# One weight piece per attention iteration, and one listed tail with filler products, in a kernel of attention, soft mixture of experts and a cosine MLP

## The chip, the cores and the metric

The kernel runs on one core of a Trainium2 chip. The metric is device time in microseconds (us) of one execution, as the median of three runs. The engines are named as in the profile: PE is TensorE's matrix products, PEld its weight loads, DVE is VectorE, ACT ScalarE, POOL GpSimd, and SP is SyncE, whose instruction queue issues all the transfers of this kernel.

## The reference

Three stages follow each other; cut to what matters:

```python
scores = q @ k.T / 8, causal mask;  attn = softmax(scores);  x = attn @ v      # 4 x 12 heads, 448 x 64
x = x as (1792 tokens, 768)
logits = x @ phi                              # 1792 x 32, 8 experts of 4 slots
d = softmax(logits, over tokens);  slot_in = d.T @ x
slot_out[e] = relu(slot_in[e] @ w1[e]) @ w2[e]   # 8 experts, 768 -> 1024 -> 768
x = softmax(logits, over slots) @ slot_out
h = x @ w_in;  out = (h * cos(h)) @ w_out        # 768 -> 2048 -> 768
```

All inputs and the output are float32. The expert weights are 50 MB, and each is read once.

## The kernel before

**Attention.** The 48 heads are worked off as 24 pairs. The tuple ORDER names the steps of one iteration, each with a lag: at iteration t, step (op, lag) works on pair t - lag, so that four pairs are in flight. S0, S1, S2 and Q3 are the score products (lines 300 and 306), sc and e the masking and the exponential (322 and 324), n the division on POOL (343), T0 and T1 the transposes of the probabilities (346), PV the product with v (390), evo the copy of its result (190), X the transposes to token rows (402). At the end of each batch of six pairs come phiA and phiB (411, 417), the logits `lg`, their replication `rep` (426), the softmax over tokens with a running maximum (dmax, dexp, dlgD, dsum), its transposition `dk` (346, on tile dT), and u0, u1 (480), which add the batch to the experts' slot inputs in `uacc` (489).

**The tail** is what the steps yield from iteration 23 on, when no pair is left to start, followed by bs0 and bs1 (the slot inputs, divided and transposed, line 502), their copy `bsc` (505) and the zeroing of two PSUM banks, mz1 and mz2 (542). The step `slots` (515 to 517) makes the divisor that bs0 reads. Before the change all of it is generated from ORDER with its lags.

**Transfers.** `run_ops` issues them from SP as soon as a step has freed their place: q and k of pair p + 2 into a buffer of two (`load_raw`, line 250) after pair p's score products, v (`load_v`, 256) after its PV. The expert weights come in 48 pieces of 1 MB (`load_piece`, 265 and 268) through a ring of 26 slots; 19 of the slots are free during attention, the other seven when the last pair's buffers are done with (the table FREE). A piece is issued with each evo, and two with those of pairs 1 and 3, until 19 are under way:

```python
            if op == "evo" and len(pieces) < NPRE:
                load_piece()
                if i in (1, 3):
                    load_piece()
```

**Experts.** A second block with a manual schedule runs the eight experts in two groups: w1 (line 761) in two halves of six pieces, w2 (776) in three of four. Each piece that PE has used frees a slot for another. The softmax of the tokens over slots (`tok_softmax`, 465 to 471) and `build_ct`, which makes the MLP's operand CT from it, are called inside this block. Two bank memsets (608) stand between the blocks. `keep_warm` (493) is a product that nobody reads; it writes bank 3 from the constants `cs`. Some stand in the last w2 products.

**MLP.** The last pieces are followed on SP by the first raw chunks of w_in and w_out (`ld`, 682), which are unpacked by ACT and DVE (689 to 700; the second chunk by `decode(1)` ahead of the last copy on ACT, 782). A planner with listed costs then sets the order of the MLP (836 to 864), where PE is busy without a break.

Of the kernel before, what the change touches and what calls it, by code (L numbers as in the profile page):

```python
# [35 lines left out]
KW = 4  # L36
HEAD = None
TH = 2
TT = 23
TAIL = None  # L40
ORDER = (
# [126 lines left out]
def moe_stack_kernel(ctx: ExitStack, tc: tile.TileContext, qk, v, cst, phi, w1, w2, w_in, w_out, out):  # L168
# [16 lines left out]
    PE, ACT, DVE, POOL, SP = nc.tensor, nc.scalar, nc.vector, nc.gpsimd, nc.sync  # L185
# [12 lines left out]
    bank = [psum.tile([128, 512], F32, name=f"bank{i}") for i in range(8)]  # L198
    TA, TB, OB, MB = bank[4:8]
# [6 lines left out]
    pslot = [slot(f"p{i}") for i in range(2)]  # L206
# [4 lines left out]
    cs = fixed.tile([128, 832], F32, name="cs")  # L211
# [4 lines left out]
    mask0 = qks[:, 1920:1984]  # L216
    rep = cs[:, 640:768]
    phs = fixed.tile([128, NPB, NS], F32, name="phs")
    ctoks = fixed.tile([128, NB * 4, NS], F32, name="ctok")
    ctok = ctoks[0:112]  # L220
    uacc = fixed.tile([128, DM], F32, name="uacc")
# [3 lines left out]
    dk = fixed.tile([128, 4, NS], F32, name="dk")  # L225
# [4 lines left out]
    b_q = fixed.tile([128, 1], F32, name="b_q")  # L230
    b_h = fixed.tile([128, 1], F32, name="b_h")
# [15 lines left out]
    @pr("load_raw")  # L247
    def load_raw(p):
        b, hp = divmod(p, NPB)
        SP.dma_start(QK(p), qk[b, hp])  # L250

    @pr("load_v")
    def load_v(p):
        b, hp = divmod(p, NPB)
        for c, n, t in VB[p % 2]:
            SP.dma_start(t, v[b, hp][:, 128 * c:128 * (c + n)])
# [3 lines left out]
    def load_piece():  # L260
        i = len(pieces)
        g, r = divmod(i, 24)
        t = slot(f"w{i}")
        if r < 12:
            SP.dma_start(t, w1[g, r // 6, r % 6])
        else:
            r -= 12
            SP.dma_start(t, w2[g, r // 4, r % 4])
        pieces.append(t)
# [221 lines left out]
    def keep_warm(n, t=cs):  # L491
        for _ in range(n):
            PE.matmul(bank[3 if t is cs else 7][:, 0:128], lhsT=t[:, 0:128], rhs=t[:, 0:128], start=True, stop=True)
# [18 lines left out]
    def slots(b):  # L512
        if b < NB - 1:
# [6 lines left out]
                T0=lambda p: t_pair(p, 0), T1=lambda p: t_pair(p, 1), PV=pv, X=x_t, evo=ev_o)  # L520
# [9 lines left out]
    for e in "AD":  # L530
        for i in range(4):
            PAIR[f"ev{i}{e}"] = lambda p, i=i, e=e: ev_t(i, e)
        for j in range(2):
            PAIR[f"evx{j}{e}"] = lambda p, j=j, e=e: ev_x(p, j, e)
    BATCH = dict(phiA=phi_a, phiB=phi_b, lg=be_logits, rep=be_rep, dmax=d_max, dexp=d_exp, dlg=lambda b: d_lg(b, "A"),
                 dlgD=lambda b: d_lg(b, "D"), dsum=d_sum, dk=be_dk, dkc=dk_c, tokc=tok_c, slots=slots)
    for h in range(2):
# [4 lines left out]
                 mz1=lambda b: DVE.memset(bank[1], 0.0), mz2=lambda b: DVE.memset(bank[2], 0.0),  # L542
# [11 lines left out]
    def all_ops():  # L554
        yield from HEAD or steps(0, TH)
        yield from steps(TH, TT)
        yield from TAIL or (*steps(TT, NPAIR + 6), ("bs0", 3), ("bs1", 3), ("bsc", 3), ("mz1", 3), ("mz2", 3))

# [5 lines left out]
    def run_ops():  # L564
        done = set()
        raws, vs = [2], [2]
        ok = lambda p, xs: all((x, p) in done for x in xs)
        for op, i in all_ops():
            (PAIR if op in PAIR else BATCH)[op](i)
            done.add((op, i))  # L570
            while raws[0] < NPAIR and ok(raws[0] - 2, ("S0", "S1", "S2", "Q3")):
                load_raw(raws[0])
                raws[0] += 1
            while vs[0] < NPAIR and ok(vs[0] - 2, ("PV",)):
                load_v(vs[0])
                vs[0] += 1
            if op == "evo" and len(pieces) < NPRE:
                load_piece()
                if i in (1, 3):
                    load_piece()  # L580
            while NPRE <= len(pieces) < NSLOT and raws[0] == vs[0] == NPAIR and done.issuperset(FREE[len(pieces) - NPRE]):
                load_piece()

    with tc.manual_schedule():
        load_raw(0)
        SP.dma_start(cs[:, 128:832], cst[:, 128:832])
        SP.dma_start(mask0, cst[:, 832:896])
        SP.dma_start(cs[:, 0:128], cst[:, 0:128])
        load_raw(1)
        load_v(0)  # L590
        load_v(1)
        SP.dma_start(phs, phi)
        DVE.memset(TA, 0.0)
        DVE.memset(TB, 0.0)
        for i in range(2):
            DVE.memset(pslot[i][:, 1984:2048], 0.0)
        DVE.memset(b_q, 0.25)
        DVE.memset(b_h, 0.5 * math.pi)
        DVE.memset(uacc[:, 0:128], 0.0)
        keep_warm(KW, uacc)  # L600
        run_ops()


    hT = dk.rearrange("p c m -> p (c m)").rearrange("p (c m) -> p c m", c=8)
    h1 = cs[:, 128:640]
    so = cs[:, 384:640]
    for i in (4, 5):
        DVE.memset(bank[i][:, 0:256], 0.0)

    def build_ct():  # L610
        ct = ex["CT"]
        ACT.activation(st[0:112, 42:43], tst[:, 16:17], AF.Sin)
# [135 lines left out]
        return t  # L748

    with tc.manual_schedule():  # L750
        for g in range(2):
            for hf in range(2):
                hb = bank[1 + hf]
                for i in range(6):
                    if (g, hf, i) == (0, 0, 2):
                        tok_softmax()
                    if (g, hf, i) == (0, 1, 3):
                        build_ct()
                    w = next_piece().rearrange("p (j f) -> p j f", j=4)
                    for j in range(4):  # L760
                        PE.matmul(hb[32 * j:32 * j + 4, :], lhsT=slotT[:, i, 16 * g + 4 * j:16 * g + 4 * j + 4],  # L761
                                  rhs=w[:, j, :], start=(i == 0), stop=(i == 5))
                ACT.activation(h1, hb, AF.Relu)
                tb = bank[3 * hf]
                for c in range(4):
                    PE.transpose(tb[:, 128 * c:128 * c + 128], h1[:, 128 * c:128 * c + 128], ident)
                DVE.tensor_copy(hT[:, 4 * hf:4 * hf + 4, :].rearrange("p c (j t) -> p c j t", j=4),
                                tb.rearrange("p (c j t) -> p c j t", c=4, j=4)[:, :, :, 0:SPE])
            for n in range(3):
                sb = bank[4 + n % 2]  # L770
                for qd in range(4):
                    w = next_piece().rearrange("p (c j f) -> p c j f", c=2, j=4)
                    for c in range(2):
                        kc = 2 * qd + c
                        for j in range(4):
                            PE.matmul(sb[32 * j:32 * j + 4, 0:256], lhsT=hT[:, kc, 4 * j:4 * j + 4], rhs=w[:, c, j, :],  # L776
                                      start=(kc == 0), stop=(kc == 7))
                    if 42 <= npc[0] < 48:
                        keep_warm(3)
                if npc[0] == 48:  # L780
                    decode(1)
                ACT.activation(so, sb[:, 0:256], AF.Copy)
                tb = bank[6]
                if npc[0] == 48:
                    keep_warm(1)
                for c in range(2):
                    PE.transpose(tb[:, 128 * c:128 * c + 128], so[:, 128 * c:128 * c + 128], ident)
                DVE.tensor_copy(soT[:, 2 * n:2 * n + 2, 16 * g:16 * g + 16].rearrange("p c (j t) -> p c j t", j=4),
                                tb[:, 0:256].rearrange("p (c j t) -> p c j t", c=2, j=4)[:, :, :, 0:SPE])
# [339 lines left out]
```

## Time and profile before

| | before |
|---|---|
| runs, us | 527.07, 527.98, 528.55 (median 527.98) |
| profiled execution, us | 527.23, span 525.4 |
| mean granted TensorE clock | 0.972 |
| busy: PE, PEld, DVE, ACT, POOL | 93%, 68%, 66%, 60%, 37% |
| chain that ended last | PE 75%, DMA 8%, DVE 8%, ACT 5% |
| transfers | 100.35 MB, 191 GB/s over the span |
| expert pieces (48 x 1024 KB) | 7.3 us from issue to landing, median |
| q and k of a pair (24 x 480 KB) | 5.5 us from issue to landing, median |

The busy share is an average over stages with different limits: attention up to about 160 us, its tail to 183, the experts to 247, the MLP to the end. The chain gives for each stretch the instruction or transfer that was waited for. [...] A row of a timeline shows the start, the length of the group, engine, line, operation and tiles, the count, and in brackets the idle time of the engine just before with what ended it.

### The profile page before, as it was taken

What the parts mean: (1) busy time and instruction counts of PE and PEld (TensorE: products, weight loads), DVE (VectorE), ACT (ScalarE), POOL (GpSimd) and SP (SyncE); (2) the same over time, 40 slices, a digit from 0 to 9 for tenths busy, and PEclk for the clock granted to TensorE, in tenths of its full rate; (3) what the DMA queues carried; (4) which work ended last, traced back from release to release, by engine and by line L of the source; (5) the groups of instructions that cost most, each with busy time, mean ns of one, the idle gap of its engine ahead of it and who ended that gap; (6) DMA issues with size and microseconds to landing.
All of it is one profiled execution on the core that took longest, in us unless ns stands there. A gap on an engine that the chain in (4) does not pass through costs nothing.

```text
span 525.4 us, 11211 instructions
## 1 busy us (share of the span) xinstructions
PE 490.2 (93%) x4234; PEld 358.5 (68%) x4234; DVE 344.3 (66%) x877; ACT 314.0 (60%) x735; POOL 196.4 (37%) x299
## 2 busy tenths in 40 slices
PE   6988999999998598888888999999999999999996
PEld 4755677677675423334766878887877787888996
DVE  4766887887884613003888899897998886445431
ACT  5878989989985111001769665747566546543552
POOL 2654556566563000000236334243433456222331
PEclk9989999999999579999899999999999999999999
DMA  5688878877328789999443434333263011213101
GB/s 195 200 334 329 302 263 278 290 278 286 111 79 304 273 324 422 418 422 415 185 181 120 131 111 129 114 120 121 81 220 120 1 61 39 82 59 129 54 1 60
DMA packets 24244, 100.35 MB, mean 191 GB/s; under 512 B 2816, under 2 KB 6912, under 8 KB 18048
## 3 DMA queue, kind: packets, MB, share of 16 engines
q1 hardware_dynamic: 24192, 99.66, 51.7%
q8 instruction: 33, 0.54, 0.4%
q14 instruction: 19, 0.16, 0.1%
HBM read 94.14 MB, written 5.51 MB: 190 GB/s over the span
## 4 chain that ended last, share of the span: by engine, by line
PE 75%; DMA 8%; DVE 8%; ACT 5%; issue 2%; POOL 0%; SPq 0%; ACTq 0%; DVEq 0%
PE bank L862 12%; PE bank L864 12%; PE bank L863 12%; PE bank L390 9%; PE bank L306 7%; PE bank L346 5%; DMA zraw<-in_w_out_dram 5%; PE bank L761 4%; DMA qk<-in_qk_dram 3%; PE bank L836 3%; PE bank L776 2%; PE bank L480 1%; PE bank L803 1%; PE bank L300 1%; DVE zscr L843 1%
## 5 line engine op out<-in xcount | busy, mean ns | idle before, releaser
L862 PE MATMUL bank<-zg,zhl 128*128 128x512 f32 (+1 forms) x378 | 139.8, 370 | 0.4 <-ACT zhl L711 0.4
L863 PE MATMUL bank<-zg,zhl 128*128 128x512 f32 (+1 forms) x378 | 137.5, 364 | 0.9 <-DVE zhl L724 0.9
L864 PE MATMUL bank<-zg,zhl 128*128 128x512 f32 (+1 forms) x378 | 137.3, 363 | 0.9 <-POOL zg L855 0.9
L855 POOL TENSOR_TENSOR zg<-zscr,zg 128x512 fp32r<-128x512 f32 (+1 forms) x64 | 82.6, 1295 | 135.9 <-ACT zg L852 121.4
L343 POOL TENSOR_SCALAR p<-p,pst 128x448 f32<-128x448 f32 (+3 forms) x168 | 82.6, 502 | 48.8 <-DVE pst L335 28.2
L324 ACT ACTIVATE p<-p,pst 128x448 f32<-128x448 f32 (+3 forms) x168 | 87.8, 524 | 13.3 <-DVE pst L322 10.9
L862 PEld LDWEIGHTS bank<-zg,zhl 128*128 128x128 f32 x378 | 71.4, 189 | 13.7 <-issue 1.2
L864 PEld LDWEIGHTS bank<-zg,zhl 128*128 128x128 f32 x378 | 71.4, 189 | 12.6 <-POOL zg L855 1.3
L863 PEld LDWEIGHTS bank<-zg,zhl 128*128 128x128 f32 x378 | 71.5, 189 | 12.4 <-DVE zhl L724 1.6
L322 DVE CUSTOM_DVE_ANT_0 p<-bank,cs 128x448 f32<-128x448 f32 (+1 forms) x96 | 52.6, 548 | 14.9 <-PE bank L300 8.5
L843 DVE SCALAR_TENSOR_TENSOR zscr<-zscr,bank 128x512 f32<-128x512 int32 (+1 forms) x64 | 38.7, 617 | 32.4 <-ACT zscr L840 32.0
L846 ACT ACTIVATE zscr<-zscr,b_h 128x512 f32<-128x512 f32 (+1 forms) x64 | 42.0, 669 | 28.8 <-DVE zscr L843 28.5
L306 PE MATMUL bank<-qk 64*128 64x192 f32 (+2 forms) x288 | 54.2, 474 | 4.3 <-DMA qk<-in_qk_dram 4.3
L852 ACT ACTIVATE zg<-zscr 128x512 fp32r<-128x512 f32 (+1 forms) x64 | 36.3, 576 | 26.0 <-DVE zscr L849 25.9
L849 DVE TENSOR_TENSOR zscr<-bank,zscr 128x512 f32<-128x512 f32 (+1 forms) x64 | 39.1, 620 | 18.3 <-ACT zscr L846 18.3
L840 ACT ACTIVATE zscr<-bank,b_q 128x512 int32<-128x512 f32 (+1 forms) x64 | 39.4, 629 | 19.6 <-PE bank L836 19.5
L724 POOL TENSOR_TENSOR zhl<-uacc,zhl 128x768 fp32r<-128x768 f32 (+1 forms) x7 | 10.8, 1548 | 105.7 <-DMA zraw<-in_w_out_dram 90.5
L689 ACT ACTIVATE zraw<-zraw 128x768 f32<-128x768 f32 x32 | 29.2, 913 | 22.6 <-DMA zraw<-in_w_in_dram 11.2
L192 DVE COPY pts<-bank 128x512 f32<-128x512 f32 x48 | 32.9, 686 | 14.3 <-PE bank L346 14.2
L346 PE MATMUL bank<-cs,p 64*128 64x64 f32 (+1 forms) x768 | 36.6, 230 | 3.8 <-POOL p L343 2.0
L346 PEld LDWEIGHTS bank<-cs,p 64*128 64x128 f32 (+1 forms) x768 | 29.4, 136 | 12.9 <-issue 4.6
L306 PEld LDWEIGHTS bank<-qk 64*128 64x128 f32 x288 | 26.7, 198 | 9.2 <-DMA qk<-in_qk_dram 4.6
(145 smaller groups left out, 699.7 us busy)
## 6 DMA issues: line engine op xcount, KB each, us to landing
w<-in_w_dram SPq DMA_DIRECT2D x48, 1024.0 KB, 7.3
zraw<-in_w_in_dram SPq DMA_DIRECT2D x16, 768.0 KB, 4.4
zraw<-in_w_out_dram SPq DMA_DIRECT2D x16, 768.0 KB, 4.3
qk<-in_qk_dram SPq DMA_DIRECT2D x24, 480.0 KB, 5.5
xk<-in_v_dram SPq DMA_DIRECT2D x12, 256.0 KB, 2.9
out_dram<-zps SPq DMA_DIRECT2D x8, 256.0 KB, 3.7
xts<-in_v_dram SPq DMA_DIRECT2D x12, 128.0 KB, 2.5
lt<-in_v_dram SPq DMA_DIRECT2D x12, 128.0 KB, 2.8
```

What stands on the lines that cost most here:

```text
L306: PE.matmul(sreg(j, c), lhsT=Q(p)[h, q0:q0 + 128], rhs=K(p)[h, 0:ln], start=True, stop=True)
L322: DVE.tensor_tensor_reduce(out=dst, in0=sb, in1=m, scale=-0.125, scalar=3.0e38, op0=ALU.add, op1=ALU.min, accum_out=st_[:, col:col + 1])
L324: return pr(f"exp{j}{c}")(lambda: ACT.activation(dst, dst, AF.Exp, bias=st_[:, col:col + 1], scale=-1.0, accum_out=st_[:, 8 + col:9 + col]))
L343: POOL.tensor_scalar(dst, dst, st_[:, 24 + col:25 + col], 0.0, op0=ALU.mult, op1=ALU.add)
L346: PE.transpose(out, src, by)
L390: PE.matmul(OB[64 * j:64 * j + 64, a:b], lhsT=V(p, c, j), rhs=r[j], start=first, stop=last)
L843: DVE.scalar_tensor_tensor(y_(s), y_(s).bitcast(I32), -2.0 * math.pi, hb[:, 0:n_(s)], op0=ALU.mult, op1=ALU.add)
L846: ACT.activation(y_(s), y_(s), AF.Sin, bias=b_h, scale=1.0)
L855: eng.tensor_tensor(g_(s)[1], y_(s), g_(s)[0].bitcast(F32), ALU.subtract)
L862: PE.matmul(o, lhsT=wh, rhs=gh, start=first, stop=False)
L863: PE.matmul(o, lhsT=wl, rhs=gh, start=False, stop=False)
L864: PE.matmul(o, lhsT=wh, rhs=gl, start=False, stop=last)
```

## The change

Three edits. The extra pieces with pairs 1 and 3 go, so that each of the first 19 evo steps issues one piece, the last with pair 18 instead of 16. TAIL, which was None, now lists all steps from iteration 23 to the start of the experts by hand. In it `slots` of the last batch stands right behind `dsum`, and three groups of fillers are added: `kwc` 8 behind `rep`, `kwc` 3 behind `dk` and `kwc` 5 behind `u1`, 16 calls of keep_warm(1) in all. The helpers of the experts move up unchanged, and the memsets of banks 4 and 5 and the experts' loop now stand inside the first manual block, so that the two are one.

```diff
-TAIL = None
+TAIL = (
...
+    ("phiB", 3), ("evx0D", 23), ("lg", 3), ("rep", 3), ("kwc", 8), ("dmax", 3), ("dexp", 3), ("dlgD", 3), ("dsum", 3),
+    ("slots", 3), ("dk", 3), ("kwc", 3), ("dkc", 3), ("tokc", 3), ("u0", 3), ("ua0", 3), ("u1", 3), ("kwc", 5),
+    ("ua1", 3), ("bs0", 3), ("bs1", 3), ("bsc", 3), ("mz1", 3), ("mz2", 3))
...
             if op == "evo" and len(pieces) < NPRE:
                 load_piece()
-                if i in (1, 3):
-                    load_piece()
...
     with tc.manual_schedule():
...
         keep_warm(KW, uacc)
         run_ops()
-
-    for i in (4, 5):
-        DVE.memset(bank[i][:, 0:256], 0.0)
...
-    with tc.manual_schedule():
+        for i in (4, 5):
+            DVE.memset(bank[i][:, 0:256], 0.0)
         for g in range(2):
             for hf in range(2):
                 hb = bank[1 + hf]
```

The order of ACT and of POOL is the same as before. Three engines' orders move. (Line numbers of the changed kernel are its own: 262 is load_raw, 268 load_v, 277 load_piece.)

SP in the first iterations: qk is q and k of a pair, xk, xts and lt receive v, w_N is a weight piece. Before:

```order
L250 DMA qk<-in_qk_dram 128x960
L256 DMA xts<-in_v_dram 128x256
L256 DMA lt<-in_v_dram 128x256
L265 DMA w_337<-in_w_dram 128x2048
L265 DMA w_339<-in_w_dram 128x2048
L250 DMA qk<-in_qk_dram 128x960
L256 DMA xk_77<-in_v_dram 128x512
L265 DMA w_435<-in_w_dram 128x2048
```

and with the change:

```order
L262 DMA qk<-in_qk_dram 128x960
L268 DMA xts<-in_v_dram 128x256
L268 DMA lt<-in_v_dram 128x256
L277 DMA w_337<-in_w_dram 128x2048
L262 DMA qk<-in_qk_dram 128x960
L268 DMA xk_77<-in_v_dram 128x512
L277 DMA w_433<-in_w_dram 128x2048
```

One piece instead of two stands ahead of this load of q and k, and the same happens once more four rows on; two pieces stand two iterations later at the end of the row of 19.

PE from `rep` to the first expert product (bank_67 is bank 3, written by the fillers). Before:

```order
L426 MATMUL bank_71<-lt,cs 128x448
L346 MATMUL bank_71<-cs,dT 112x128 x4
L480 MATMUL bank_71<-xk_77,dk 32x128 x12
L480 MATMUL bank_69<-xk_78,dk 32x128 x12
L502 MATMUL bank_64<-pst_87,uacc 128x32 x6
L761 MATMUL bank_65<-w_240,phs 4x512 x4
```

and with the change (505 is keep_warm, each of these rows counts two passes on the engine):

```order
L438 MATMUL bank_71<-lt,cs 128x448
L505 MATMUL bank_67<-cs 128x128 x8
L358 MATMUL bank_71<-cs,dT 112x128 x4
L505 MATMUL bank_67<-cs 128x128 x3
L492 MATMUL bank_71<-xk_77,dk 32x128 x12
L492 MATMUL bank_69<-xk_78,dk 32x128 x12
L505 MATMUL bank_67<-cs 128x128 x5
L514 MATMUL bank_64<-pst_87,uacc 128x32 x6
L767 MATMUL bank_65<-w_240,phs 4x512 x4
```

Only the three groups of fillers are new; the order of the rest stands.

DVE from `dsum` on, where 515 to 517 are `slots`, 465 to 471 the softmax of the tokens over slots, 489 the additions to uacc, 505 the copy of the slot inputs. Before:

```order
L450 SCALAR_TENSOR_TENSOR st<-st 128x1
L457 COPY dk<-bank_71 112x128
L460 COPY ctok<-bank_71 112x128
L465 TENSOR_REDUCE pst_88<-ctok 112x16
L466 TENSOR_TENSOR ctok<-ctok,pst_88 112x512
L489 SCALAR_TENSOR_TENSOR uacc<-uacc,st,bank_71 128x384
L489 SCALAR_TENSOR_TENSOR uacc<-uacc,st,bank_69 128x384
L515 TENSOR_SCALAR st<-st 128x1
L468 TENSOR_REDUCE pst_88<-ctok 112x16
L516 RECIPROCAL st<-st 128x1
L608 MEMSET bank_69 128x256
L517 TENSOR_SCALAR pst_87<-cs,st 128x32
```

and with the change:

```order
L462 SCALAR_TENSOR_TENSOR st<-st 128x1
L527 TENSOR_SCALAR st<-st 128x1
L528 RECIPROCAL st<-st 128x1
L529 TENSOR_SCALAR pst_87<-cs,st 128x32
L469 COPY dk<-bank_71 112x128
L472 COPY ctok<-bank_71 112x128
L501 SCALAR_TENSOR_TENSOR uacc<-uacc,st,bank_71 128x384
L501 SCALAR_TENSOR_TENSOR uacc<-uacc,st,bank_69 128x384
L517 COPY phs<-bank_64 128x192
L554 MEMSET bank_65 128x512
L554 MEMSET bank_66 128x512
```

The divisor is made before the transposes are copied, and the tokens' softmax with its six instructions now comes behind the copy of the slot inputs and four memsets.

## Rows read from the trace of the kernel before

**Rows 1.** PE's waits from 12 to 60 us: in total, times, longest (us).

```profile
PE bank L306 <- DMA qk<-in_qk_dram: 4.3, 2, 2.3
```

**Rows 2.** Timeline of SP, its issues around 25 us (start, length).

```profile
24.89 0.99 SPq L265 DMA_DIRECT2D w<-in_w_dram  x2
26.07 0.33 SPq L250 DMA_DIRECT2D qk<-in_qk_dram  x1
```

**Rows 3.** The loads of q and k (line 250), whole span.

```profile
DMA to landing us min/median/max: 3.3/5.5/8.8
```

**Rows 4.** Timeline of PE: the first score product of pairs 5 and 7.

```profile
34.91 1.25 PE L306 MATMUL bank<-qk 64*128 64x448 f32 x4 [2.27 <-DMA qk<-in_qk_dram]
...
50.25 1.02 PE L306 MATMUL bank<-qk 64*128 64x448 f32 x4 [2.03 <-DMA qk<-in_qk_dram]
```

**Rows 5.** Busy time by stretch: length; PE to POOL; granted clock, DMA share, GB/s.

```profile
26.72:55.99 29.27, 24.97 (x327) 16.36 (x322) 19.25 (x87) 23.23 (x74) 15.92 (x37) 0.94 0.85 321
69.67:94.37 24.70, 24.70 (x347) 17.61 (x344) 19.91 (x89) 23.31 (x75) 15.94 (x37) 1.00 0.81 286
34.91:42.65 7.74, 7.74 (x83) 4.36 (x83) 3.63 (x17) 4.01 (x13) 2.59 (x6) 0.78 0.60 197
76.19:82.84 6.65, 6.65 (x87) 4.48 (x85) 5.58 (x27) 6.52 (x22) 4.53 (x10) 1.00 0.73 243
```

**Rows 6.** Timeline of PE, the tail from rep to the first expert product.

```profile
169.88 1.02 PE L426 MATMUL bank<-lt,cs 128*128 128x448 f32 x2 [0.66 <-ACT lt L422]
173.22 1.10 PE L346 MATMUL bank<-cs,dT 128*112 128x128 f32 x4 [2.32 <-DVE dT L192]
174.89 2.79 PE L480 MATMUL bank<-xk,dk 112*32 112x128 f32 x48 [0.58 <-DVE ctok L460]
179.55 2.77 PE L502 MATMUL bank<-pst,uacc 128*128 128x32 f32 x12 [1.87 <-DVE pst L469]
183.36 1.03 PE L761 MATMUL bank<-w,phs 128*4 128x512 f32 x4 [1.04 <-DVE bank L542]
```

**Rows 7.** Busy time by stretch in tail and experts, columns as in rows 5.

```profile
169.00:172.50 3.50, 1.23 (x10) 0.30 (x2) 1.00 (x3) 1.40 (x5) 0.00 (x0) 0.95 1.04 370
172.50:183.40 10.90, 6.70 (x68) 5.54 (x72) 6.86 (x19) 0.82 (x3) 0.00 (x0) 0.50 0.71 261
...
184.00:187.00 3.00, 3.00 (x20) 0.59 (x16) 0.00 (x0) 0.00 (x0) 0.00 (x0) 0.50 0.30 52
187.00:247.50 60.50, 54.37 (x640) 22.17 (x632) 10.50 (x26) 6.59 (x12) 0.00 (x0) 0.98 1.01 418
```

**Rows 8.** Timeline of SP: the pieces issued in the tail and at the experts' start.

```profile
176.46 1.64 SPq L265 DMA_DIRECT2D w<-in_w_dram  x2
...
185.30 2.04 SPq L265 DMA_DIRECT2D w<-in_w_dram  x2
```

**Rows 9.** The chain that ended last, and ACT's timeline, at the MLP's start.

```profile
228.19 19.34 DMA zraw<-in_w_out_dram
...
247.55 0.92 ACT L689 ACTIVATE zraw<-zraw 128x768 f32<-128x768 f32 x1 [7.63 <-DMA zraw<-in_w_out_dram]
```

**Rows 10.** Timeline of PE at the higher clock: dk, half of u, w1 pieces, fillers.

```profile
63.61 0.65 PE L346 MATMUL bank<-cs,dT 128*112 128x128 f32 x4
...
66.64 0.86 PE L480 MATMUL bank<-xk,dk 112*32 112x128 f32 x24
...
192.87 2.76 PE L761 MATMUL bank<-w,phs 128*4 128x512 f32 x24
...
255.88 1.39 PE L493 MATMUL bank<-cs 128*128 128x128 f32 x11
```

**Rows 11.** Timeline of DVE in the tail.

```profile
177.75 0.62 DVE L489 SCALAR_TENSOR_TENSOR uacc<-uacc,st,bank 128x384 f32<-128x384 f32 x1 [0.66 <-PE bank L480]
...
179.32 0.17 DVE L517 TENSOR_SCALAR pst<-cs,st 128x32 f32<-128x32 f32 x1
...
179.84 0.69 DVE L471 TENSOR_TENSOR ctok<-ctok,pst 112x512 f32<-112x512 f32 x1
```

More of the change, by code (lines that the diff above doesn't have):

```diff
@@ L578, in run_ops @@
                 load_piece()
-                if i in (1, 3):
-                    load_piece()
             while NPRE <= len(pieces) < NSLOT and raws[0] == vs[0] == NPAIR and done.issuperset(FREE[len(pieces) - NPRE]):
                 load_piece()
-    with tc.manual_schedule():
[L585 to L601, printed above, removed]
     hT = dk.rearrange("p c m -> p (c m)").rearrange("p (c m) -> p c m", c=8)
@@ L750, in moe_stack_kernel @@
     with tc.manual_schedule():
+        load_raw(0)
+        SP.dma_start(cs[:, 128:832], cst[:, 128:832])
+        SP.dma_start(mask0, cst[:, 832:896])
+        SP.dma_start(cs[:, 0:128], cst[:, 0:128])
+        load_raw(1)
+        load_v(0)
+        load_v(1)
+        SP.dma_start(phs, phi)
+        DVE.memset(TA, 0.0)
+        DVE.memset(TB, 0.0)
+        for i in range(2):
+            DVE.memset(pslot[i][:, 1984:2048], 0.0)
+        DVE.memset(b_q, 0.25)
+        DVE.memset(b_h, 0.5 * math.pi)
+        DVE.memset(uacc[:, 0:128], 0.0)
+        keep_warm(KW, uacc)
+        run_ops()
+        for i in (4, 5):
+            DVE.memset(bank[i][:, 0:256], 0.0)
         for g in range(2):
```

9 rows, old and new, of the table TAIL are left out of this document.

## The prediction, made before the changed kernel was run

> **What bounds the kernel now.** PE is busy 93% of the span, so I looked first for the stretches where it is not, or where its clock is down. There are two. The list of PE's waits shows, in the first 60 us, one releaser that isn't an engine: the score products waited twice for a load of q and k, 4.3 us in all [rows 1]. SP's timeline says why: two weight pieces of 1 MB were issued 1.2 us ahead of that load [rows 2], which then took 8.8 us to land, the longest of the 24, against a median of 5.5 [rows 3]. PE's timeline puts the waits ahead of pairs 5 and 7 [rows 4], the first pairs loaded after the two double issues (pairs 1 and 3).
>
> The second stretch is the tail. [...] PE's timeline shows a chain of small steps, each waiting for DVE: dk 2.32 us, u 0.58, the slot products 1.87, the experts 1.04 [rows 6].
>
> What makes these waits count is the stage behind them. From 187 to 247.5 us the DMA engines are full at 418 GB/s [rows 7], and the MLP starts when the second raw chunk lands: it was issued at 228.19, landed 19.34 us later behind pieces still under way, and ACT had waited 7.63 us for it [rows 9]. So between tail and MLP the kernel is bound by transfers, and a faster tail helps by as much as it starts that stream earlier. The stream starts when PE has used its first piece: the issue at 185.30 [rows 8], 1.94 us after the first expert product at 183.36 [rows 6]. Just before, from 184 to 187, the DMA share was 0.30 [rows 7]: there the queue was short of work, so an earlier issue is not wasted. From the MLP on nothing is edited, and I let it move as a block.
>
> **The front: one piece instead of two.** From the first score product of pair 4 to that of pair 8 took 29.27 us, at a clock of 0.94. The same places in the next batch, pairs 10 to 14, took 24.70 at clock 1.00 [rows 5], and they hold 0.86 us of u1 products [rows 10] that the first batch doesn't have: 23.84 us. The difference is **5.4 us**. It can be worked out the other way: the two waits, 2.27 + 2.03 [rows 4], and the lower clock behind the first, 7.74 us from pair 5 to 6 against 6.65 one batch later [rows 5], 1.1: again 5.4. The batches behind already issue one piece per iteration and show no such wait, which is why I take all of it. The check on pair 5: PE was ready for it at 34.91 - 2.27 = 32.64, which is 6.6 us after the issue at 26.07; with one piece ahead the median landing is 5.5 [rows 2, 3], so 1.1 us are spare. Bounds: 4.3 if the clock's share isn't saved, 5.4 at most. SP also issues one transfer less ahead of those loads; that is inside the 5.4. The two pieces put off go out with pairs 17 and 18, in iterations that had none, where they meet what other iterations carry without waiting (DMA share 0.81, clock 1.00 [rows 5]); they are used some 40 us later. I cost them at nothing; if they made one qk late, it would cost about 2 us once.
>
> **The tail.** All times are those of the trace before, without the front's shift. `rep` ends at 170.90 [rows 6]. A filler is two passes of 1.39 / 11 = 0.126 us at the higher clock [rows 10].
> - Eight fillers take 2.0 us and end at 172.9, inside the 2.32 us that PE waited for DVE: dk still starts at 173.22. They cost nothing and keep PE at work. At the higher clock dk takes 0.65 instead of 1.10 [rows 6, 10] and ends at 173.9.
> - Three fillers, 0.8 us, end at 174.6. Meanwhile DVE copies dk and ctok, 0.6 us. So u starts at 174.6, 0.2 later than it could, and still 0.3 earlier than before.
> - u0 and u1 take 2 x 0.86 = 1.7 instead of 2.79 [rows 6, 10]: done at 176.35. The two pieces that wait for their buffers move from 176.46 [rows 8] to about 175.6.
> - Five fillers, 1.3 us, end at 177.6, while DVE adds, 0.62 each, until about 177.0 [rows 11]. They hold the slot products up by 0.6.
> - Before, those waited till 179.5 for the divisor (L517 at 179.32), which stood behind instructions of the tokens' softmax although uacc was ready at 178.37 [rows 11]. Now the divisor is made right behind `dsum`, in time in which DVE waits for dk. So they start at 177.65. Twelve passes at 0.126 are 1.5 us instead of 2.77 [rows 6]: done at 179.15 instead of 182.32.
> - The copy and the first memset stay, 1.04 us [rows 6]: the experts start at 180.2, 3.2 earlier. A first piece of eight passes takes 8 x 2.76 / 24 = 0.9 us [rows 10], and the next issue comes about 1.1 us after the start instead of 1.94: at 181.3, **4.0 us** earlier.
>
> From this I take off 0.3 us, because the two pieces of 176.46 move only 0.9 and now run into the new ones: **3.7 us**. Bounds: 3.2, what the experts' start alone gives, and 4.4, if the fillers between cost nothing. The tokens' softmax, now behind the memsets, has four DVE instructions about as long as L471's 0.69 us [rows 11], two small ones and one on ACT: some 4 us under the first six pieces, which take PE 48 x 2.76 / 24 = 5.5 us [rows 10]; nothing waits for it before build_ct's transposes, three pieces later. The memsets of banks 4 and 5 lie there too, long before w2 uses them. If that cover failed, the first copy behind it on DVE would come late by the overhang, and PE, which runs ahead of the transfers here, could lose that.
>
> PE itself must follow. Its experts started 3.2 earlier and the first half gains the lower clock's share on top, so it is ahead of the transfers by more than before, and they stay the bound. What is late next is the second raw chunk, as now [rows 9].
>
> **Sum.** 5.4 + 3.7 = 9.1 us off. The profiled execution took 527.23, 0.75 under the median of the runs; against it the sum is 518.1. The four executions shown have a mean of 527.7, and I take that as the base of a median: **518.6 us**. The forecast's own range goes from 516.6 (5.4 and 4.4, and 1 us for the spread of executions) to 520.6 (4.3 and 3.2, with the same).
>
> **Rivals.**
> - *The clock falls before the first filler.* Between 168 and 170.9 PE has gaps of its own, 0.66 us among them [rows 6]. If the clock is down when the fillers start, they take double, 4 us, and push dk to 174.9; with the durations of rows 6 the slot products end at 185.6, and the stream starts 3.2 us later than before: 525.5 if it stays down throughout. But PE now works without a break, and after the fall behind pair 5 the clock was back within the iteration (0.78 over it [rows 5]); if it returns halfway, the tail comes out about even: 522. Against it speaks that the clock fell only after 1.7 us of idleness behind `rep` had joined the earlier gaps [rows 6, 7]. [...] Chance 0.12.
> - *One wait in front stays.* The spare 1.1 us are less than the landing times scatter [rows 3]. One wait with its clock is 2.3 + 1.1: 522.0. Chance 0.08.
> - *The tail's gain ends at another wait*, because the stream is not what the MLP waits for once it comes earlier, or PE takes its place: 527.7 - 5.4 = 522.3. Against it: 7.63 us of ACT's waiting [rows 9]. Chance 0.05.
> - *Slower: one piece per iteration is already too much.* Without the waits the pairs follow faster, and if every load of q and k then lands later than the 6.6 us that are there, PE waits in each of some 17 iterations, the front gains nothing, and each microsecond over costs 17. It breaks even with the tail's 3.7 at a landing of 6.8 us; at 7.5 us it is 527.7 - 3.7 + 15.3 = 539. Against it: iterations from 56 us on do carry a piece each, at full clock and without a gap [rows 5], with a median landing of 5.5 [rows 3]. Chance 0.02.
>
> **How the numbers follow.** The forecast has 0.73. The range of 8 in 10 reaches from its lower end over most of the cases that give 522: 516.6 to 522.0. Outside lie the clock that stays down, the slower rival, and some scatter. A measurement of this kernel can tell about 0.3%, 1.6 us, from no change; all cases but the last give more than that unless two come together: faster 0.95, same 0.03, slower 0.02.
>
> **What would show it.** Right: no wait of PE for q and k in the first 60 us, and 23.5 to 24.5 us from pair 4 to pair 8 at clock 1.00; granted clock 1.00 from rep to the experts, dk at 0.65 and the u products at 1.7 us; the slot products starting at uacc and not at the divisor; from the end of rep to the first expert product 9.3 us instead of 12.5; the DMA engines full from about 1 us after that; the second raw chunk landing about 9 us earlier, and the MLP as long as before. Wrong: a clock of 0.50 anywhere between rep and the first half of w1, fillers of 0.5 us, qk landings over 6.6 us with a wait behind, or a raw chunk that lands earlier while ACT or DVE start on it no sooner.

## The result, and the profile after

The changed kernel takes **521.6 us** (median of four runs, 521.30 to 521.62), beside 528.3 for the kernel before, measured with it: a ratio of 0.9875, 95% interval 0.9857 to 0.9894. The forecast was 518.6, its range 516.6 to 522.0, so the time lies inside the range, at its upper end, and above the 520.6 at which the forecast's own range ended. The profiled execution took 521.58 us (span 519.8, mean granted clock 0.990 of full speed), 5.65 less than that of before. The medians are 6.7 apart; the sum had said 9.1.

**Front.** The list of PE's waits from 12 to 160 us no longer names a load of q and k [rows 1]; these are all its rows of 0.4 us and more:

```profile
PE bank L358 <- ACT pts L202: 1.3, 3, 0.5
PE bank L358 <- DVE pts L204: 0.4, 1, 0.4
```

Busy time from the first score product of pair 4 to that of pair 8, columns as in rows 5:

```profile
26.62:50.53 23.91, 23.91 (x328) 17.03 (x322) 19.36 (x89) 23.20 (x75) 16.05 (x37) 1.00 0.87 310
```

23.91 us against 29.27, without a gap and at clock 1.00.

**Tail.** PE's timeline from rep (438) on, to hold beside rows 6; 505 are the fillers, 358 is dk, 492 u, 514 the slot products, 767 the experts:

```profile
164.36 1.02 PE L438 MATMUL bank<-lt,cs 128*128 128x448 f32 x2 [0.66 <-ACT lt L434]
165.22 1.95 PE L505 MATMUL bank<-cs 128*128 128x128 f32 x16
167.70 0.65 PE L358 MATMUL bank<-cs,dT 128*112 128x128 f32 x4 [0.54 <-DVE dT L204]
168.18 0.83 PE L505 MATMUL bank<-cs 128*128 128x128 f32 x6
169.11 1.52 PE L492 MATMUL bank<-xk,dk 112*32 112x128 f32 x48
170.56 1.38 PE L505 MATMUL bank<-cs 128*128 128x128 f32 x10
171.78 1.42 PE L514 MATMUL bank<-pst,uacc 128*128 128x32 f32 x12
174.24 2.81 PE L767 MATMUL bank<-w,phs 128*4 128x512 f32 x15 [1.04 <-DVE bank L554]
```

From rep's start to the first expert product it is 9.88 us; before it was 13.48. DVE's timeline shows the divisor (its last step, line 529) done long before the slot products, and uacc ready at 171.31 (170.04 + 1.27):

```profile
168.31 0.24 DVE L529 TENSOR_SCALAR pst<-cs,st 128x32 f32<-128x32 f32 x1
...
170.04 1.27 DVE L501 SCALAR_TENSOR_TENSOR uacc<-uacc,st,bank 128x384 f32<-128x384 f32 x2 [0.99 <-PE bank L492]
```

**Transfers behind it.** Busy time in the tail, at the experts' start, and in the stream, columns as in rows 5:

```profile
164.36:174.24 9.88, 8.21 (x98) 7.15 (x99) 4.73 (x13) 0.91 (x3) 0.00 (x0) 1.00 0.81 299
175.20:178.60 3.40, 3.40 (x24) 0.68 (x20) 2.49 (x7) 0.63 (x1) 0.00 (x0) 0.52 1.01 381
174.00:182.00 8.00, 7.04 (x49) 1.45 (x49) 4.25 (x10) 1.27 (x3) 0.00 (x0) 0.79 0.96 337
186.00:239.50 53.50, 46.08 (x575) 19.80 (x573) 8.96 (x19) 4.49 (x9) 0.00 (x0) 1.00 1.01 419
```

The clock is 1.00 through the whole tail and falls only in the first expert products (0.52 from 175.20 to 178.60), behind slot products and a gap of 1.04. The DMA engines are full at once (a share of 0.96), but for the first 8 us they move 337 GB/s and not 419. SP's issues at the experts' start, and ACT's decode of the second raw chunk (rows 8 and 9 of before):

```profile
175.40 4.55 SPq L277 DMA_DIRECT2D w<-in_w_dram  x4
```

```profile
239.57 0.91 ACT L676 ACTIVATE zraw<-zraw 128x768 f32<-128x768 f32 x1 [9.46 <-DMA zraw<-in_w_out_dram]
```

The first issue is 9.9 us earlier than the one at 185.30 [rows 8], the decode 8.0 us earlier than at 247.55 [rows 9].

**MLP.** From that decode to the end of the span it is now 519.8 - 239.57 = 280.2 us; before, 525.4 - 247.55 = 277.9. It gives back 2.4 us, and two places show up when both traces are laid on the decode. The first is DVE's shift for weight chunk 16 (679; before 692) beside POOL's subtraction (861; before 855). Before, DVE was first:

```profile
321.30 0.54 DVE L692 TENSOR_SCALAR zfa<-zraw 128x768 int32<-128x768 int32 x1
322.17 1.30 POOL L855 TENSOR_TENSOR zg<-zscr,zg 128x512 fp32r<-128x512 f32 x1 [2.21 <-ACT zg L852]
```

Now POOL is first by 0.07 us, and the shift takes 1.63:

```profile
312.78 1.29 POOL L861 TENSOR_TENSOR zg<-zscr,zg 128x512 fp32r<-128x512 f32 x1 [1.27 <-PE bank L870]
312.85 1.63 DVE L679 TENSOR_SCALAR zfa<-zraw 128x768 int32<-128x768 int32 x1
```

The second is a raw chunk that came late:

```profile
388.77 0.88 ACT L676 ACTIVATE zraw<-zraw 128x768 f32<-128x768 f32 x1 [2.34 <-DMA zraw<-in_w_in_dram]
```

What each place costs is read at PE's products, whose order is the same in both kernels, counted from the decode. Behind the long shift PE waits where it did not wait before; the row of before first, 83.94 us behind its decode, then that of the change, 84.37:

```profile
331.49 0.63 PE L836 MATMUL bank<-CT,zWS 96*128 96x512 f32 x2
```

```profile
323.94 0.73 PE L842 MATMUL bank<-CT,zWS 96*128 96x512 f32 x2 [0.76 <-DVE zWS L828]
```

Three products ahead of this wait PE was 0.5 us sooner than before, three products behind it 0.5 us later: the place costs 1.0 us. The late chunk, read in the same way at PE's next long wait, costs 1.5 us:

```profile
389.97 0.67 PE L820 MATMUL bank<-cs 128*96 128x256 f32 x2 [1.21 <-ACT cs L817]
```

So in this execution: front 5.5, tail 2.5 (8.0 - 5.5), MLP -2.4; together the 5.6 that were measured.

### The profile page after: what moved, and what is told of

Same layout as the page of the kernel before. It is cut to its first block, busy times and chain, and to the rows that moved or that the text cites. A ratio compares the mean times of both kernels' runs of the same rounds, so it can differ in the third digit from the quotient of the medians.

```text
span 519.8 us, 11277 instructions
## 1 busy us (share of the span) xinstructions
PE 489.4 (94%) x4266; PEld 359.6 (69%) x4266; DVE 345.6 (66%) x877; ACT 313.5 (60%) x735; POOL 196.6 (38%) x299
## 4 chain that ended last, share of the span: by engine, by line
PE 66%; DMA 14%; DVE 11%; ACT 6%; issue 1%; POOL 0%; ACTq 0%; SPq 0%
PE bank L868 10%; PE bank L870 10%; PE bank L869 10%; PE bank L402 10%; PE bank L318 8%; DMA w<-in_w_dram 7%; PE bank L358 6%; DMA zraw<-in_w_out_dram 5%; PE bank L842 2%; DMA zraw<-in_w_in_dram 2%; PE bank L767 2%; DVE zscr L849 2%; DVE zscr L855 2%; ACT zraw L676 1%; PE bank L312 1%
## 5 line engine op out<-in xcount | busy, mean ns | idle before, releaser
L676 ACT ACTIVATE zraw<-zraw 128x768 f32<-128x768 f32 x32 | 29.1, 910 | 26.4 <-DMA zraw<-in_w_in_dram 14.6
L336 ACT ACTIVATION_READ_ACCUMULATOR p<-p,pst 128x1 f32 x168 | 31.6, 188 | 0.0
```

The source lines that it names most:

```text
L336: return pr(f"exp{j}{c}")(lambda: ACT.activation(dst, dst, AF.Exp, bias=st_[:, col:col + 1], scale=-1.0, accum_out=st_[:, 8 + col:9 + col]))
```

## Experiments

Two theories at first. **A**: front and tail add up, and the MLP's loss is an accident of timing at the two places. **B**: the MLP gives back whatever the tail gains. The table gives, for each profile, the time from rep to the first expert product, from there to the decode of the second raw chunk, and from the decode to the end of the span, each the difference of two rows as above. Its last two columns are the lengths of two DVE steps in the MLP: the shift for weight chunk 16, and the step of line 683 (696 before) that is the subject of the experiment without fillers.

| kernel | rep to experts | experts to decode | decode to end | chunk-16 shift | step 683 |
|---|---|---|---|---|---|
| before | 13.48 | 64.2 | 277.9 | 0.54 | 0.96 |
| front only | 13.49 | 65.5 | 278.1 | 0.54 | 0.96 |
| tail only | 9.89 | 64.4 | 279.4 | 1.38 | 0.96 |
| no fillers | 11.55 | 64.5 | 279.9 | 0.54 | 2.63 |
| the change | 9.88 | 65.3 | 280.2 | 1.63 | 0.96 |
| the change again | 9.88, 9.88 | 64.4, 65.9 | 279.8, 280.7 | 1.34, 1.60 | 0.96, 2.47 |
| clock held | 9.88 | 65.1 | 279.6 | 1.46 | 2.55 |
| fillers elsewhere | 11.54 | 64.3 | 280.2 | 1.61 | 0.96 |
| shift first | 9.88, 9.89 | 65.5, 63.8 | 277.5, 278.0 | 0.55, 0.55 | 0.96, 0.96 |
| clock held and shift first | 9.89 | 65.2 | 278.5 | 0.55 | 0.96 |
| piece behind q and k, shift first | 9.89 | 65.4 | 278.8 | 0.55 | 0.96 |
| late divisor, shift first | 9.94 | 64.7 | 278.9 | 0.55 | 0.96 |

**The front alone**: the kernel before, without the second piece.

```diff
-                if i in (1, 3):
-                    load_piece()
```

> The kernel before with one edit: one weight piece per evo step, tail and blocks as before. Theory A (front and tail add up; the 2.4 us that the MLP of the changed kernel lost are accidents of its timing): no wait for q and k in the first 60 us, 23.9 us from pair 4 to pair 8, the second raw chunk 5.5 us earlier than before, and the whole 5.5 us (4.5 to 6) at the end, so about 1 us slower than the whole change. Theory B (the MLP gives back whatever the tail gains): also 5.5 us, but then equal to the whole change within 0.3 us. If the front were worth less by itself, under 4.5 us.

Measured: 0.9929 of before (0.9903 to 0.9956), 524.9 us, so 3.7 us. Three waits for q and k stayed, 1.39, 0.41 and 0.39 us.

**The tail alone**: the changed kernel with those two lines put back.

> The whole change with the extra pieces of pairs 1 and 3 put back. Both: the two waits for q and k are there again, 4.3 us. Theory A: the second raw chunk lands 2.5 us earlier than before and the time is 1 to 3 us under before. Theory B: the raw chunk lands 2.5 us earlier, and the time is that of before within 0.5 us, since the MLP takes 2.5 us longer.

Measured: 0.9940 (0.9911 to 0.9969), 526.4 us: 3.2 us by the ratio, 2.1 by the medians. The two parts add up to 0.987, and the whole change is at 0.9875: as far as these intervals can tell, neither eats the other's gain. From rep to the decode (the table's second and third column together) it is 77.7 and 79.0 us with the old tail, and 74.9 in the mean of the ten profiles with the new one and its fillers: a gain of 3.4, near the 3.7 of the sum. But from the decode on, this kernel and the change with its repeats are 1.4 to 2.7 us longer than the 278.0 of the two profiles with the old tail.

**No fillers**: the changed kernel without its three groups of `kwc`.

```diff
-    ("phiB", 3), ("evx0D", 23), ("lg", 3), ("rep", 3), ("kwc", 8), ("dmax", 3), ("dexp", 3), ("dlgD", 3), ("dsum", 3),
-    ("slots", 3), ("dk", 3), ("kwc", 3), ("dkc", 3), ("tokc", 3), ("u0", 3), ("ua0", 3), ("u1", 3), ("kwc", 5),
+    ("phiB", 3), ("evx0D", 23), ("lg", 3), ("rep", 3), ("dmax", 3), ("dexp", 3), ("dlgD", 3), ("dsum", 3),
+    ("slots", 3), ("dk", 3), ("dkc", 3), ("tokc", 3), ("u0", 3), ("ua0", 3), ("u1", 3), 
```

> The whole change without the sixteen fillers: the divisor and the tokens' softmax stay where the change puts them. Both: the clock falls in the tail as before, dk takes 1.1 us and the slot products 2.8; they start about 1.2 us earlier than before (counted from rep), since they no longer wait for the divisor. The stream of pieces starts 1.2 us plus the front's 5.5 earlier than before. Theory A: the raw chunk 6.7 us earlier than before, time 521.5 to 523. Theory B: the same time as the whole change, 521.6, within 0.4.

Measured: 522.3 us, 0.9885 (0.9855 to 0.9916), not to be told apart from the whole change. PE's timeline:

```profile
170.61 2.79 PE L492 MATMUL bank<-xk,dk 112*32 112x128 f32 x48 [0.58 <-DVE ctok L472]
173.33 2.77 PE L514 MATMUL bank<-pst,uacc 128*128 128x32 f32 x12
177.14 7.81 PE L767 MATMUL bank<-w,phs 128*4 128x512 f32 x48 [1.04 <-DVE bank L554]
```

u and slot products take 2.79 and 2.77, as in rows 6, but the slot products no longer wait 1.87. So of the 3.6 us by which the experts start earlier, 1.9 come from the order of the steps and 1.7 from the fillers.

The chunk-16 shift was short here, and yet the MLP took 1.9 us longer than with the old tail. 1.1 of it stands at a second near tie of the same two engines, 14.6 us ahead of the shift: POOL subtracts (711), DVE unpacks another weight chunk (683). In the changed kernel DVE was first:

```profile
299.59 0.96 DVE L683 SCALAR_TENSOR_TENSOR zfb<-zraw,zfb 128x768 int32<-128x768 int32 x1
299.72 2.54 POOL L711 TENSOR_TENSOR zhl<-lt,zhl 128x768 fp32r<-128x768 f32 x1 [6.43 <-ACT zhl L698]
```

Without the fillers POOL was, by 0.03 us; DVE's step took 2.63, and PE waited for DVE where it had no wait with the change:

```profile
302.35 1.84 POOL L711 TENSOR_TENSOR zhl<-lt,zhl 128x768 fp32r<-128x768 f32 x1 [6.28 <-ACT zhl L698]
302.38 2.63 DVE L683 SCALAR_TENSOR_TENSOR zfb<-zraw,zfb 128x768 int32<-128x768 int32 x1
...
307.45 0.50 PE L842 MATMUL bank<-CT,zWS 96*128 96x512 f32 x1 [0.87 <-DVE zscr L855]
```

In two other profiles POOL was first here as well, the change's second repeat and the clock held alone. In these three the place costs PE's products 1.0 to 1.1 us, counted from the decode as above, in the eleven others nothing.

**The change again**, twice, on two chips:

> The changed kernel once more, for a second profile of it. Theory A: the second raw chunk lands within 0.5 us of 239.5, but the MLP behind it shows other losses than the first profile (there a DVE shift of 1.63 us instead of 0.54 beside POOL, and a raw chunk that landed 6.8 us after its issue), and its length differs by over 0.5 us. Theory B: the same losses at the same places, MLP as long as in the first profile within 0.3 us.

> The changed kernel unchanged, on the chip of these runs, for what the three others are compared with. All theories: 0.985 to 0.99 of the kernel before; no wait for q and k over 0.5 us; from decode to the last back product 275.2 to 275.8 us, with the shift at 1.3 to 1.7 us beside POOL.

Measured: 520.7 (one run), and 521.1 at 0.9876 (0.9845 to 0.9907). The shift was the longer one both times, 1.34 and 1.60 us; the late chunk was less late, ACT waited 1.26 and 1.28 us for it instead of 2.34 (0.79 before). Waits for q and k did, 0.4 and 2.5 us in all: the rival that one front wait stays is true of some executions.

**The clock held** through the gap ahead of the experts, alone and with the swap of the next experiment:

```diff
-    ("ua1", 3), ("bs0", 3), ("bs1", 3), ("bsc", 3), ("mz1", 3), ("mz2", 3))
+    ("ua1", 3), ("bs0", 3), ("bs1", 3), ("kwc", 4), ("bsc", 3), ("mz1", 3), ("mz2", 3))
```

> Four more fillers (8 passes, 1 us at the higher clock) go behind the slot products, into the 1.04 us in which PE waits for the first copy and the memset before the experts. Nothing else is changed. Theory A (the stream of pieces that the tail starts is held back because the clock falls into the first expert products: PE there frees a piece per 1.7 us, and the DMA engines, with one or two loads under way, moved 324 to 360 GB/s instead of 418 for 8 us): the granted clock stays 1.00 from 175 to 179 us, the pieces behind the first are issued some 0.8 us apart instead of 1.7, the stretch from 174 to 182 us moves over 380 GB/s, and the second raw chunk is 0.5 to 1.5 us earlier from rep: 73.0 us from rep to ACT's decode instead of 74.1. The time is that much lower unless the MLP gives it back. Rival A2 (the rate there is what the DMA engines give with the small loads, or PE's clock is not what holds the issues back): clock 1.00, but rep to decode stays at 74.1 within 0.3. Theory B (the MLP gives back what the tail gains): decode earlier, MLP longer by as much, time unchanged within 0.3 us.

> The four fillers ahead of the experts and the swap in the MLP together. Theory A: the two gains add up, 1.3 to 2.6 us under the unchanged kernel beside it. Theory B: no gain within 0.5 us, because the MLP ends at the same time whatever comes before it.

Measured: 521.2 us, 0.9865 (0.9830 to 0.9901), and 519.9, 0.9849 (0.9819 to 0.9880): no gain beside their unheld partners, 521.1 and 518.4. The clock did stay up; busy time at the experts' start of the first of them:

```profile
175.50:182.00 6.50, 5.72 (x52) 1.37 (x51) 4.32 (x10) 1.41 (x3) 0.00 (x0) 1.00 0.89 331
```

and the transfers moved 331 GB/s all the same. Rival A2 holds: here PE's clock is not what holds the stream back. In all fourteen profiles, whatever the tail and the clock, the decode comes 63.8 to 65.9 us behind the first expert product.

**The shift first**: one swap in the planner's finished list, run twice.

```diff
+    x = [n for n, p in enumerate(plan) if p[2] == ("l", 16)][0]
+    y = max(n for n in range(x) if plan[n][3] == "D")
...
+    plan.insert(y, plan.pop(x))
     bk = lambda t: bank[6 + hbo[t]]
```

> One swap in the MLP's list and nothing else: DVE's shift for weight chunk 16 goes ahead of the addition of an output part that stood before it, so that it starts some 0.6 us earlier, ahead of POOL's subtraction beside which it took 1.34 to 1.63 us in the three kernels with the fillers, and 0.54 in the three without them. Theory A (the MLP's loss is a near tie of DVE and POOL at this place, plus late weight loads): the shift takes 0.54 us, POOL's subtraction may take 1.6 instead of 1.3, and from decode to the last back product it is some 0.8 to 1.1 us shorter than in the unchanged kernel beside it (275.3 to 275.7): 274.2 to 274.9. The time falls by 0.8 to 1.1 us. Theory B (the MLP gives back what the tail gains, whatever happens at this place): the shift may be short, but the 275.3 stay within 0.3, since another wait takes its place.

> The swap in the MLP alone, again, for comparison on this chip. Theory A: 518 to 520 us, shift of chunk 16 at 0.55 us, 273 to 274 us from decode to the last back product; some q and k waits of 0 to 2.5 us.

Measured: 518.4 us (518.35 to 520.16), 0.9821 (0.9793 to 0.9848), and on another chip 518.7, 0.9817 (0.9778 to 0.9856). DVE is first now, and in the first of the two profiles neither is held up (in the second POOL took 1.38):

```profile
311.83 0.55 DVE L679 TENSOR_SCALAR zfa<-zraw 128x768 int32<-128x768 int32 x1
...
312.28 1.30 POOL L861 TENSOR_TENSOR zg<-zscr,zg 128x512 fp32r<-128x512 f32 x1 [1.19 <-PE bank L870]
```

From decode to end the five profiles with the swap have a mean of 278.3 us, the six with a shift of 1.3 us or more 280.0, where the old tail had 278.0. Theory B falls: nothing takes the shift's place. But the race at chunk 16 is only 0.9 of these 1.7 us: around PE's wait behind it the six lose 0.7 to 1.1 us, counted from the decode as above, and the eight profiles with a short shift at most 0.04. The rest lies at other places, among them the second tie, which comes ahead of the swapped step: two of the six lost it, and none of the five. These are the two fastest medians of the study. That the first lies 2.7 us under the change measured beside it, and not 0.9, is not explained by the swap; both profiles also had no fall of the clock in the first 19 us (below).

**Fillers elsewhere**: no fillers in the tail, and the same 16 products (32 passes) in the experts' second group.

```diff
+                    if (g, hf) == (1, 0) and i < 4:
+                        keep_warm(4)
```

> The kernel without the tail's fillers, with the same 16 products put into the experts' first half of the second group, four behind each of four pieces, where PE waits for transfers anyway. It has as many PE instructions ahead of the MLP as the changed kernel, and the tail without fillers (experts some 11.1 us behind rep instead of 9.4). Theory F (the 32 more PE instructions move the transfers that fetch PE's instructions, and those transfers decide which of DVE and POOL starts first at weight chunk 16): the fetch lies at about 63 us behind the decode of chunk 1 and not at 68 to 70, chunk 16 is there 4.1 to 4.4 us after its issue and not 4.6 or more, POOL's subtraction starts ahead of DVE's shift, and the shift takes 1.3 to 1.7 us. Rival G (the fillers or the earlier tail itself decide it): fetch at 63, but the shift takes 0.54 as in the kernel without fillers.

Measured: the shift takes 1.61 us, behind POOL by 0.09:

```profile
321.35 1.28 POOL L863 TENSOR_TENSOR zg<-zscr,zg 128x512 fp32r<-128x512 f32 x1 [1.25 <-PE bank L872]
321.44 1.61 DVE L679 TENSOR_SCALAR zfa<-zraw 128x768 int32<-128x768 int32 x1
```

The instruction queue of the DMA engines carried its transfer 64.0 us behind the decode, and ACT could start on chunk 16 4.42 us after its issue. In the three kernels without the 32 passes this transfer comes at 68 to 70, within chunk 16's flight, which takes 4.56 to 5.38 us; in all eleven profiles with them it comes at 62 to 64, and the flight takes 4.12 to 4.44. That fits theory F: not the fillers' place but their number decides, as far as one execution can tell. The chunk comes sooner, ACT and POOL with it, and without the swap POOL wins the race by 0.07 to 0.37 us. That the instruction transfer itself is what holds the chunk up rests on their times alone. This single execution took 528.9 us: PE waited 3.5 us for q and k, once 2.50, and its tail was slow (11.54 us from rep to the experts); that says nothing of the race. Nor did PE wait for transfers where the fillers went, as the expectation had it: it had no such wait there with the change either, and here it ended its last expert products at 249.5, behind the decode at 246.94. So part of this kernel's 280.2 is PE's lateness, not the race.

**Piece behind q and k**, with the swap:

```diff
             while raws[0] < NPAIR and ok(raws[0] - 2, ("S0", "S1", "S2", "Q3")):
                 load_raw(raws[0])
                 raws[0] += 1
+                if raws[0] > NPAIR - NPRE:
+                    load_piece()
...
-            if op == "evo" and len(pieces) < NPRE:
-                load_piece()
```

> The swap in the MLP, and each weight piece of the attention issued right behind the load of q and k instead of ahead of it, from pair 5's load on. Theory A (what is left of the front's waits comes from the piece that stands ahead of each q and k load): no wait for q and k over 0.2 us in the whole attention, landings of q and k near 4.5 us or under, and rep 159.5 to 160.0 us behind the first score product in every execution (the swap alone had 159.8, the changed kernel 160.5 to 162.9). The time is some 0.5 to 2 us under the swap alone in the median, and it scatters less. Rival (the waits come from the loads of v or from the rate of the chip's memory): waits of 0.5 to 2.5 us remain; or the loads of v come late instead and PE waits for them in PV.

Measured: no wait for q and k over 0.2 us and a median landing of 3.7 us, as expected of the waits. Yet 519.3 us (517.5 to 522.1), 0.9817 (0.9773 to 0.9861), the same as the swap alone beside it, and it scatters more, not less. The forecast for the time was a miss. So was the one for rep, which came 161.5 us behind the first score product, 1.3 to 2.2 later than with the swap alone; this execution had the clock at 0.50 from 15 to 19 us (last section).

**Late divisor**, with the swap: `slots` moved behind `ua1`.

```diff
-    ("slots", 3), ("dk", 3), ("kwc", 3), ("dkc", 3), ("tokc", 3), ("u0", 3), ("ua0", 3), ("u1", 3), ("kwc", 5),
-    ("ua1", 3), ("bs0", 3), ("bs1", 3), ("bsc", 3), ("mz1", 3), ("mz2", 3))
+    ("dk", 3), ("kwc", 3), ("dkc", 3), ("tokc", 3), ("u0", 3), ("ua0", 3), ("u1", 3), ("kwc", 5),
+    ("ua1", 3), ("slots", 3), ("bs0", 3), ("bs1", 3), ("bsc", 3), ("mz1", 3), ("mz2", 3))
```

> The swap in the MLP, and the divisor's three instructions behind the second addition of the tail again instead of behind dsum. As the prediction has it (the early divisor is worth what the slot products waited for it): the three take DVE 0.3 to 0.7 us behind the second addition, which ends about when the five fillers do, so the slot products start 7.4 to 7.7 us behind rep instead of 6.94, the experts 9.9 to 10.2 instead of 9.4, and the raw chunk comes as much later, which the scatter of +-0.8 us may hide. Rival (the divisor was never what ended that wait): slot products at 6.94 still.

Measured: 520.2 us (one run); the experts start 9.94 us behind rep instead of 9.88, so the rival holds. DVE's divisor and PE's next row:

```profile
171.94 0.24 DVE L529 TENSOR_SCALAR pst<-cs,st 128x32 f32<-128x32 f32 x1
```

```profile
172.24 1.53 PE L514 MATMUL bank<-pst,uacc 128*128 128x32 f32 x12
```

The divisor ends at 172.18, under the last fillers. What had made it late before was the tokens' softmax ahead of it [rows 11]; with that moved away, its place is free.

## Why the prediction was right, and where it was off

That the time fell into the range was in part luck. The forecast's own range ended at 520.6; worked out from its terms it is 516.9 to 521.2 (527.7 less 9.8 and less 7.5, and 1 us more each way). It was stretched to 522.0 for rivals with a wait left in front or an end to the tail's gain. In the profiled execution no wait was left in front. Of the 3.5 us that it lacks against the sum, 2.4 were lost in the MLP, which the sum had at nothing, and 1.2 in the tail; the front gave 0.1 more.

- **Front, 5.4 us: right** in the profiled execution (29.27 to 23.91, both waits and the lower clock gone), an upper end on average. The spare 1.1 us that the check on pair 5 found are less than the landings scatter: nine of the eleven other profiles with one piece per iteration had waits for q and k, 0.4 to 3.5 us in all. Run alone the front was worth 3.7.
- **Tail, experts 3.2 us earlier: right, 3.6.** dk took 0.65 and u 1.52 at full clock, and the slot products started at 171.78, at the end of their fillers and 0.5 us behind uacc. The divisor's own place, which the step credited, is worth 0.06; the softmax taken from ahead of it is what counted.
- **The cover held.** The tokens' softmax ran on DVE from 175.2 to 179.2 us, before the first copy of the experts, which nothing delayed.
- **The stream starts 4.0 us earlier, less 0.3: the right size on average, by a wrong step.** The issue came 4.4 us earlier, but the gain does not follow it. The decode lies about 65 us (63.8 to 65.9) behind the experts' start in all kernels, because the transfers left at that point fill that time; what counts is the experts' start, the lower bound of the step. In the profiled execution the overlap cost 1.9 us instead of 0.3. At the experts' start 1.3 MB more were left to move than before (410 GB/s over 65.33 us against 397 over 64.19), and for the first 8 us the DMA engines moved 337 GB/s while they were full (0.96). Over the profiles the tail comes out at 3.4.
- **"I let it move as a block": the step that failed.** The MLP gave back 2.4 us in the profiled execution and 2.0 on average over the six profiles with a long shift. In the profiled execution the race of DVE and POOL at chunk 16 is 1.0 of it and the late chunk 1.5. Over the six the race is 0.9, and with the swap it is gone. The second tie of the same two engines takes another 1.0 to 1.1 in the profiles in which POOL is first there; it is over half of what the kernel without fillers lost, whose shift was short. The rest is not laid to one cause, and why a raw chunk lands late in single executions was not tried.
- **The rival that the clock falls before the first filler: wrong.** It was 1.00 in the tail of every profile with the fillers. (Before, it had fallen 1.2 us behind rep and not 1.7, as the text against this rival has it: 0.95 over the 3.5 us of rows 7 puts the fall at 172.15, and rep ends at 170.90.) Behind the gaps of 0.66 and 0.54 us in the tail of the change the clock stayed up. Behind the 1.04 us in front of the experts it fell in six of the eight profiles that have it behind fillers (0.52 from 175.2 to 178.6 in the profiled execution of the change); in the change's second repeat and the second run of the shift first, with the same instructions, it did not (1.00 in both).
- **The slower rival: wrong**, by a wide margin: where the loads of q and k had one piece ahead of them, the sum of PE's waits for them was at most 3.5 us.

## What to carry to other kernels

A stage that nobody edits can't be taken to move as a block where two engines that hold each other up start within a few tenths of a microsecond (DVE and POOL here: POOL first by 0.03 to 0.37 us, DVE's step then 0.8 to 1.7 us longer); look for such pairs in the trace before and order them by hand. Idle work for PE in a tail is worth what the next bound stage starts earlier, and no more: here that was 1.7 us at the experts' start, which the runs could not tell from nothing, and holding the clock further, into a stage bound by transfers, bought nothing (521.2 us beside 521.1). Put loads that are waited for ahead of bulk loads in a queue, but expect gain only where the wait shows: here no wait over 0.2 us was left, and the time was the same (519.3 us beside 518.7).

## What the runs showed that was not expected

**DVE and POOL held each other up for almost whole instructions.** Alone, the shift takes 0.54 us and the subtraction 1.30. When POOL was first by 0.07, the shift ended 0.41 us behind POOL's end (312.85 + 1.63 against 312.78 + 1.29). In all six profiles in which POOL was first, by 0.07 to 0.37 us, the shift ended 0.41 or 0.42 us behind it. When DVE was first by 0.07 or 0.08 us (no fillers, front only), POOL took 1.63 and 1.62, and ended 1.16 us behind the shift's end. So the one that starts second ends as if it waited for the other's end, but for 0.12 to 0.14 us by which it ends sooner than its own length behind that. What it is that the one waits for, no run shows.

**Full DMA engines do not always move the same.** A share of 0.96 stood beside 337 GB/s over 8 us at the experts' start, one of 1.01 beside 419 later. PE's clock isn't it, since with the clock held at 1.00 the rate was no higher (331 GB/s over 6.5 us, against 342 over the like 6.5 us of the change); what it is stays open.

**In the ramp of the pipeline the clock differs between executions.** Up to the first weight piece, 18 us or more into the span, all these kernels run the same instructions, and yet the clock in the first 19 us differed. Busy time of the shift-first kernel's second run, and then of the one with the piece behind q and k, columns as in rows 5:

```profile
9.00:15.00 6.00, 3.04 (x47) 2.25 (x48) 4.59 (x24) 5.58 (x21) 4.50 (x10) 1.00 0.33 102
15.00:19.00 4.00, 4.00 (x52) 2.54 (x50) 3.05 (x13) 3.79 (x13) 2.96 (x8) 1.00 0.26 99
```

```profile
9.00:15.00 6.00, 3.22 (x46) 2.34 (x43) 4.30 (x23) 5.38 (x20) 4.35 (x10) 0.82 0.30 94
15.00:19.00 4.00, 4.00 (x22) 1.60 (x21) 2.48 (x12) 2.73 (x9) 2.00 (x5) 0.50 0.24 90
```

Three of the fourteen profiles stayed at 1.00, three fell to 0.50 from 15 to 19 us, and the others to 0.72 to 0.76 before that. Counted from its first score product, the second of these two is 2.5 us later at that of pair 4 than the first. This is more than the race at chunk 16 costs, so a microsecond between the medians of two kernels here is not yet a difference between them.
